# Attention and channel mix on one core: raw weight blocks move into spare tiles, the first queries come in two pieces, half of an early V product moves into other PSUM banks

## The chip, the cores and the metric

The kernel runs on one core of one Trainium2 chip. The core has five engines: PE (TensorE, matrix products), DVE (VectorE), ACT (ScalarE), POOL (GpSimd) and SP (SyncE, which issues the DMAs here). The metric is the device time of one execution in microseconds (us).

## What is computed

The inputs are q, k and v of 8 batches x 8 heads x 576 tokens x 64, and the weights of a channel mix. Both parts are float32.

```python
def _attn_ref(q, k, v):
    # rotate(x): rotary embedding, x1*cos - x2*sin and x1*sin + x2*cos over the halves of the 64
    q_rot, k_rot = (rotate(q), rotate(k))
    scores = scale * np.matmul(q_rot, k_rot.transpose(0, 1, 3, 2))
    scores = scores - np.max(scores, axis=-1, keepdims=True)
    attn = np.exp(scores)
    attn = attn / (np.sum(attn, axis=-1, keepdims=True) + 1e-09)
    return np.matmul(attn, v).astype(np.float32)

def _moe_ref(x, mu_k, mu_r, w_k, w_v, w_r):      # x: the heads side by side, 8 x 576 x 512
    x_prev = np.concatenate([np.zeros((B, 1, D), dtype=np.float32), x[:, :-1, :]], axis=1)
    xk = mu_k * x + (1.0 - mu_k) * x_prev
    xr = mu_r * x + (1.0 - mu_r) * x_prev
    k = np.maximum(xk @ w_k, 0.0)                # w_k: 512 x 1024
    v = k * k @ w_v                              # w_v: 1024 x 512
    r = 1.0 / (1.0 + np.exp(-(xr @ w_r)))        # w_r: 512 x 512
    return (r * v).astype(np.float32)
```

The weights reach the kernel as 64-bit numbers; it turns them into a high and a low float32 part itself.

## The kernel before, in words

**Attention.** Two heads make a pair, four pairs a batch, 32 pairs in all. For a pair, `plan_rope` loads keys (`xk`, 128x576, in two versions) and queries (`xq`, 128x640, in two versions) into tiles `nat`, multiplies them with the table `turn` in two products and adds them up into `kh` and `qh`. For the first nine pairs ("plain") this is all; later pairs get a high and a low part of both (`kh`, `kl`, `qh`, `ql`). `plan_unit` makes the scores in five units of 128 query columns: PE writes a tile `s` of two PSUM banks for each head (L431; the fifth unit has one tile), DVE takes the negated maximum `nm` (L440), ACT the exponentials into `p` with their sums (L444), and DVE transposes `p` in place (L447). `plan_ratio` makes the reciprocals of the sums, `rs` and `rw`. `plan_values` multiplies with V: 144 products per pair into two tiles `av` that are taken from the `s` family (L500), then 8 that spread the reciprocals (L506). `plan_total` copies these out with ACT (`rp`), multiplies with DVE (L531) and gets the head outputs `xT0` and `xT1`, one per half of the tokens.

PSUM has eight banks: three `s` tiles of two banks, and two `acc` tiles of one bank for the products of the channel mix.

**Weights.** `plan_convert` turns one block of 128x512 weights into its two parts. It loads the raw 64-bit block (`raw`, L339), ACT takes two signed parts of the top bits (`we`, `wm`, L345), DVE or POOL subtracts them (`wm<-we,wm`), ACT scales the middle bits (`we`, L351), POOL adds them (`wm<-wm,we`), ACT or DVE casts to the high part (`wk_h`, `wr_h`, `wv_h`, L312 or L314), and DVE or POOL subtracts for the low part (`wk_l`, `wr_l`, `wv_l`). There are 8 blocks of w_k, 4 of w_r and 8 of w_v, and one tile each of `raw`, `we` and `wm`. All the products, sums and differences with two SBUF inputs are recorded by the helper `combine`, so they have one line, L308.

**Channel mix.** For each batch and each half of the tokens, `plan_mix` mixes a pair's output with that of the token before into `mxf` (L571 or L569, then L574) and splits it into `mxh` and `mxl`; `plan_product` sums three products per pair or block into `acc` (L599 to L601); `plan_key`, `plan_gate` and `plan_value` square, gate and store.

**Order.** Every step is an `op` with a rank. `Plan.issue` keeps, for each engine, a list of steps whose inputs and tiles are there, always takes the one of the lowest rank, and so fixes the order of instructions of every engine when the program is built. Ranks come from a table of numbers: `R` for kinds of steps, `PB` and `EARLY` for the first pairs, `WORDS` for the weight blocks, `MB` for the batches; the `B_` numbers say how readily DVE takes a step that ACT or POOL could do, and `WAIT` how much a step of DVE or POOL that needs the port they share is put off while the other engine holds it. `BUFS` has the number of tiles of each family. A tile's next user waits for its last one.

Of the kernel before, what the change touches and what calls it, by code (L numbers as in the profile page):

```python
# [25 lines left out]
R = dict(k=41.29, q=43.11, v=-208.71, cs=-1094.85, ld=858.21, rope0=735.67, rope1=1324.78, rope2=-1784.84,  # L26
         split0=-295.59, split1=1862.14, u0=-14.6, u1=-12.59, u2=0.4, u3=-11.84, u4=-9.27, mx=-84.96, ex=99.42,
         rz=-275.08, rs=-668.43, dg=-117.58, bd=451.61, tr=-238.29, ev=349.84, av=10.21, av2=287.22, tot=-501.88,
         bor=-905.72, m0=174.53, mh=-2.54, mk=-24.02, mr=-14.79, ms=1.64, tp=850.66, rc=-602.82, mx1=-206.82,
         mx2=-1085.1, mx3=812.05, mg=3.33, mv=0.11, dr=-1034.03, key0=1074.87, key1=-426.54, key2=117.33,  # L30
         gate0=-493.48, gate1=383.07, wk0=120.98, wk1=45.04, wr0=-1131.23, wr1=-1623.73, wv0=98.26, wv1=1824.21)
# [15 lines left out]
WORDS = dict(wk=(-412.27, 471.27, -302.28, -396.61, -1095.29, -563.8, -1080.79, -139.77), wr=(-436.28, -440.01,
             -795.2, 242.23), wv=(-475.45, -213.94, -422, -856.83, -795.63, -590.27, 613.81, -729.62))
CY = 12
CUTS = (0, 6, 12, 18)  # L50
WAIT = 10.29
BUFS = dict(nat=2, kh=2, kl=2, qh=2, ql=2, vs=1, pt=2, s=3, nm=6, sums=2, rs=2, rw=1, rp=2, xT0=4, xT1=4, last=5, raw=1, we=1, wm=1, mxf=2, mxh=5, mxl=5, acc=2, hr=2, kkh=8, kkl=8, rt=3)
# [206 lines left out]
def rope_attention_channel_mix(ctx, tc, qt, kt, v, cs, mu, w_k, w_v, w_r, out):  # L259
# [72 lines left out]
    def plan_convert(t, src, hi, lo):  # L332
        d = {}
        s_w, s_e, s_m = Slot("raw"), Slot("we"), Slot("wm")

        def load():
            words = sb.tile([P, 513, 2], U32, tag="raw", name="raw", bufs=BUFS["raw"])
            quarters = words.rearrange("p n w -> p (n w)").bitcast(I16)
            nc.sync.dma_start(quarters[:, 1:2049], src)  # L339
            d["middle"] = words[:, 0:512, 1]  # L340
            d["top"] = quarters.rearrange("p (n w) -> p n w", w=4)[:, 1:513, 0]

        def signed(n, scale):
            d[n] = sb.tile([P, 512], I32, tag="w" + n, name="w" + n, bufs=BUFS["w" + n])
# [6 lines left out]
        e = op("A", t, act(512) + 30, lambda: A.mul(d["e"], d["middle"], 2.0 ** -13), [m], [s_w, s_e])  # L351
# [17 lines left out]
    def plan_rope(t, d, n, src, plain, pi):  # L369
# [4 lines left out]
        def load():  # L374
            m["x"] = sb.tile([P, 2, SQ], F32, tag="nat", name="x" + n, bufs=BUFS["nat"])
            m["c"], m["s"] = m["x"][:, 0, 0:w], m["x"][:, 1, 0:w]
            nc.sync.dma_start(m["x"][:, :, 0:w], src)
# [4 lines left out]

        ld = dma(t + R["ld"], P * 8 * w, load, [], [slot])
        ms = op(two(w, B_ROPE), t + lead("rope0", pi), 0, lambda e: combine(e, m["s"], m["s"], turn[:, 1, 0:w], ALU.mult), [ld] + tables["cs"], [slot])
        mc = op(two(w, B_ROPE), t + lead("rope1", pi), 0, lambda e: combine(e, m["c"], m["c"], turn[:, 0, 0:w], ALU.mult), [ld] + tables["cs"], [slot])
        sh = d["s" + n + "h"] = Slot(n + "h")
        if plain:
            r = op(two(w, B_ROPE), t + lead("rope2", pi), 0, lambda e: combine(e, f32(part(n + "h")), m["c"], m["s"], ALU.add), [ms, mc], [slot, sh])
            d[n], d["s" + n] = [r], [sh]
            return  # L390
# [24 lines left out]
    def plan_unit(t, d, c):  # L415
# [17 lines left out]
        m = op("T", t, (8 if d["plain"] else 6) * (120 + 12), products, d["q"] + d["k"], slots + d["sq"] + d["sk"], ("row" if c < 4 else "full", (8 if d["plain"] else 12) * len(heads)))  # L433
# [47 lines left out]
    def plan_values(t, d):  # L481


        w, slots = {}, [Slot("s"), Slot("s")]
# [4 lines left out]
        def at(a, x, c0):  # L489
            return w[a % 2][(up, dn)[x], a // 2, c0:c0 + Q]  # L490

        def values(b0, b1):
            if b0 == 0:
                for half in range(2):
                    w[half] = ps.tile([P, 2, 512], F32, tag="s", name="av", bufs=BUFS["s"])
# [22 lines left out]
        for half in range(2):  # L518
            plan_total(t, d, half, w, slots[half], o)

    def plan_total(t, d, half, w, slot, o):
# [3 lines left out]
        def copied():  # L525
            w["r", half] = sb.tile([P, 2, N // 2], F32, tag="rp", name="rp", bufs=BUFS["rp"])
            A.copy(w["r", half], w[half][:, :, 256:256 + N // 2])  # L527

        def total():
            x = d["x", half] = sb.tile([P, N + 1], F32, tag=f"xT{half}", name=f"xT{half}", bufs=BUFS[f"xT{half}"])  # L530
            V.tensor_tensor(out=x[:, 1:N + 1].rearrange("p (c n) -> p c n", c=2), in0=w[half][:, :, 0:N // 2], in1=w["r", half], op=ALU.mult)  # L531
# [10 lines left out]
        o = op("A", t + lead("rc", d["pi"]) + 0.1 * half, act(288) + 60, copied, [o], [slot, s_r])  # L542
        o = op("V", t + lead("tot", d["pi"]) + 0.1 * half, dve(288) + 30, total, [o], [slot, s_r, sx])
# [223 lines left out]
```

## Time and profile before

| | us |
|---|---|
| median of 3 runs | 992.77 (991.27 to 993.28) |
| the profiled execution | 991.33 |
| its span, first to last instruction | 989.6 |
| PE busy | 928.9 |
| DVE busy | 772.8 |
| ACT busy | 569.9 |
| POOL busy | 509.0 |

The span is what the profiler saw of the profiled execution; the 1.7 us to its own time lie around it. Busy times are sums over the span. What an engine waited for is inferred from the semaphores. The granted clock of PE is a share of full speed. A score unit or a weight product stands in the trace as two matmuls for each float32 instruction, and some records can be missing.

### The profile page before, as it was taken

Reading aid. Unit: us, or ns where it says so; the run is one execution under the profiler, and the core shown is the slowest. Engines: PE = TensorE matmul, PEld = TensorE weight load, DVE = VectorE, ACT = ScalarE, POOL = GpSimd, SP = SyncE. Lnnn points to the kernel's source line nnn. Section 1 sums busy time; section 2 is a strip of 40 time slices with the busy share of each in tenths; the row PEclk is TensorE's granted clock in tenths of the full one; section 3 lists DMA queues with packets and bytes.
Section 4 is the critical chain, followed back from the end, with each engine's and each line's share of the span. In section 5 each row is a group of like instructions: output and inputs, shape, how many; then the busy total and the mean of one; then the engine's idle time right before and its main releaser. Section 6 shows DMA issues by size and latency. Waiting matters only on the chain.

```text
span 989.6 us, 34384 instructions
## 1 busy us (share of the span) xinstructions
PE 928.9 (94%) x15134; PEld 821.1 (83%) x15134; DVE 772.8 (78%) x1248; ACT 569.9 (58%) x1394; POOL 509.0 (51%) x547
## 2 busy tenths in 40 slices
PE   2676789999999999999999999999999999999998
PEld 1344568888988999889988998988988999899998
DVE  5978789997786969788796969888696869874652
ACT  4655578355674747465574747566564737543343
POOL 6647677465653647465563647455463637131211
PEclk9867779999999999999999999999999999999999
DMA  7336532323333222233333222233322222111000
GB/s 254 123 114 217 179 121 93 126 101 112 112 112 112 97 78 101 70 106 112 112 107 105 94 92 79 90 110 107 118 107 84 86 100 78 59 62 57 20 25 25
DMA packets 30453, 100.38 MB, mean 101 GB/s; under 512 B 3040, under 2 KB 11232, under 8 KB 26208
## 3 DMA queue, kind: packets, MB, share of 16 engines
q1 hardware_dynamic: 30304, 98.19, 28.5%
q8 instruction: 118, 1.93, 0.8%
q14 instruction: 31, 0.25, 0.1%
HBM read 88.74 MB, written 9.44 MB: 99 GB/s over the span
## 4 chain that ended last, share of the span: by engine, by line
PE 82%; DVE 8%; ACT 4%; issue 2%; DMA 2%; POOL 1%; SPq 0%; DVEq 0%; ACTq 0%; POOLq 0%
PE acc L599 19%; PE av L500 16%; PE s L431 15%; PE acc L600 15%; PE acc L601 15%; DVE nm L440 2%; DVE mxf L574 2%; ACT p L444 1%; DVE p L447 1%; DMA raw<-in_w_k 1%; PE av L506 1%; DMA xk<-in_kt 1%; DMA raw<-in_w_v 1%; ACT rt L646 1%; DVE xq L308 1%
## 5 line engine op out<-in xcount | busy, mean ns | idle before, releaser
L444 ACT ACTIVATE p<-s,nm 128x576 f32<-128x576 f32 x288 | 211.7, 739 | 104.2 <-DVE nm L440 102.9
L440 DVE TENSOR_REDUCE nm<-s 128x1 f32<-128x576 f32 x288 | 202.2, 735 | 14.6 <-PE s L431 14.0
L447 DVE STREAM_TRANSPOSE p<-p 128x576 f32<-128x576 f32 x288 | 208.2, 752 | 2.5 <-ACT p L444 2.0
L500 PE MATMUL av<-p,values 32*64 32x144 f32 x9216 | 179.6, 293 | 13.9 <-issue 9.8
L500 PEld LDWEIGHTS av<-p,values 32*64 32x64 f32 x9216 | 151.7, 133 | 34.3 <-issue 25.6
L431 PE MATMUL s<-kh,qh 64*128 64x288 f32 (+1 forms) x738 | 145.3, 433 | 35.7 <-ACT p L444 16.7
L599 PE MATMUL acc<-mxh,wk_h 128*128 128x288 f32 x512 | 162.7, 318 | 1.7 <-ACT hr L616 1.5
L599 PE MATMUL acc<-kkh,wv_h 128*128 128x288 f32 x512 | 158.6, 310 | 4.1 <-DVE rt L655 4.0
L601 PE MATMUL acc<-mxh,wk_l 128*128 128x288 f32 x512 | 152.4, 298 | 1.9 <-DVE wk_l L308 1.9
L600 PE MATMUL acc<-mxl,wk_h 128*128 128x288 f32 x512 | 152.4, 298 | 0.0
L600 PE MATMUL acc<-kkl,wv_h 128*128 128x288 f32 x512 | 151.3, 296 | 0.0
L601 PE MATMUL acc<-kkh,wv_l 128*128 128x288 f32 x512 | 151.0, 295 | 0.0
L431 PEld LDWEIGHTS s<-kh,qh 64*128 64x128 f32 (+1 forms) x738 | 80.3, 207 | 83.6 <-ACT p L444 26.6
L308 POOL TENSOR_TENSOR mxl<-mxf,mxh 128x288 fp32r<-128x288 f32 x87 | 78.0, 903 | 74.9 <-ACT mxh L312 33.9
L308 POOL TENSOR_TENSOR kkl<-hr,kkh 128x288 fp32r<-128x288 f32 x99 | 87.6, 890 | 56.3 <-ACT kkh L312 45.0
L599 PEld LDWEIGHTS acc<-mxh,wk_h 128*128 128x128 f32 x512 | 97.0, 189 | 19.6 <-issue 13.6
L599 PEld LDWEIGHTS acc<-kkh,wv_h 128*128 128x128 f32 x512 | 96.1, 188 | 17.5 <-issue 11.5
L655 DVE TENSOR_TENSOR rt<-acc,rt 128x288 f32<-128x288 f32 x64 | 29.0, 453 | 101.5 <-PE acc L601 99.5
L527 ACT COPY rp<-av 128x288 f32<-128x288 f32 x64 | 22.4, 402 | 145.7 <-PE av L506 145.7
L538 POOL COPY last<-xT 128x1 f32<-128x1 f32 x32 | 6.9, 217 | 191.0 <-DVE xT L531 190.9
L601 PEld LDWEIGHTS acc<-mxh,wk_l 128*128 128x128 f32 x512 | 97.4, 190 | 2.1 <-DVE wk_l L308 2.1
L600 PEld LDWEIGHTS acc<-mxl,wk_h 128*128 128x128 f32 x512 | 97.4, 190 | 0.4
(86 smaller groups left out, 1921.5 us busy)
## 6 DMA issues: line engine op xcount, KB each, us to landing
values<-in_v SPq DMA_DIRECT2D x32, 1152.0 KB, 5.6
xq<-in_qt SPq DMA_DIRECT2D x32, 640.0 KB, 5.2
xk<-in_kt SPq DMA_DIRECT2D x32, 576.0 KB, 4.2
out_dram<-rt SPq DMA_DIRECT2D x64, 144.0 KB, 1.8
raw<-in_w_k SPq DMA_DIRECT2D x8, 512.0 KB, 3.6
raw<-in_w_v SPq DMA_DIRECT2D x8, 512.0 KB, 3.6
raw<-in_w_r SPq DMA_DIRECT2D x4, 512.0 KB, 4.2
turn<-in_cs SPq DMA_DIRECT2D x1, 640.0 KB, 4.9
```

The lines of the kernel that those rows point to most:

```text
L308: (V if e == "V" else G).tensor_tensor(out=out, in0=a, in1=b, op=op)
L431: T.matmul(w[x][:, h, 0:H], lhsT=kind(d[q][r, c * P:(c + 1) * P]), rhs=kind(d[k][r, h * H:(h + 1) * H]), start=i == 0, stop=i == len(todo) ...
L440: V.tensor_reduce(out=w["nm", x], in_=w[x][:, :, 0:H], op=ALU.max, axis=AX.XY, negate=True)
L444: A.activation(out, w[x][:, :, 0:H].rearrange("p a (b n) -> p a b n", n=32), AF.Exp, bias=w["nm", x], scale=1.0, accum_out=d["sums"][:, pl ...
L447: V.transpose(queries(d, place), queries(d, place))
L500: T.matmul(at(a, x, 0), lhsT=d["vf"][g, b * P + x * D:b * P + x * D + D], rhs=d["pt"][g, b, x * Q:x * Q + Q], start=b == 0, stop=b == NB - 1)
L527: A.copy(w["r", half], w[half][:, :, 256:256 + N // 2])
L574: V.scalar_tensor_tensor(out=x["f"], in0=d["x", half][:, 1:1 + n], scalar=mu_t[:, m:m + 1], in1=x["f"], op0=ALU.mult, op1=ALU.add)
L599: T.matmul(w["a"], lhsT=w_h[:, i, sl], rhs=x["h"], start=(i == 0), stop=False)
L600: T.matmul(w["a"], lhsT=w_h[:, i, sl], rhs=x["l"], start=False, stop=False)
L601: T.matmul(w["a"], lhsT=w_l[:, i, sl], rhs=x["h"], start=False, stop=(i == count - 1))
L655: o = op("V", t + R["dr"], dve(n), lambda: V.tensor_tensor(out=x["r"], in0=w["a"], in1=x["r"], op=ALU.mult), [done, o], [s_a, s_r])
```

## The change

There are three changes in the code, and a new table of numbers.

1. `plan_convert` takes its raw block from the tile family `ql` and its first signed part from `kl`, which the plain pairs leave unused and of which there are two each; `raw` and `we` are gone, and `wm` has two tiles. So two blocks can be under way.
2. The queries of the first pair are loaded in two pieces, columns 0 to 127 and 128 to 639, with their own products and sums. A unit of a plain pair asks for the pieces that it reads (`d["q"][:c + 1]`).
3. For the first four pairs, the V product of the second half of the tokens goes to the two `acc` tiles instead of a second `s` tile. ACT's copy and DVE's multiplication of that half become two each, one per bank.

```diff
-R = dict(k=41.29, q=43.11, v=-208.71, cs=-1094.85, ld=858.21, rope0=735.67, rope1=1324.78, rope2=-1784.84,
+R = dict(sg=146.09, k=35.07, q=51.6, v=-92.97, cs=-1440.03, ld=485.93, rope0=775.97, rope1=1341.24, rope2=-1593.82,
...
-WAIT = 10.29
-BUFS = dict(nat=2, kh=2, kl=2, qh=2, ql=2, vs=1, pt=2, s=3, nm=6, sums=2, rs=2, rw=1, rp=2, xT0=4, xT1=4, last=5, raw=1, we=1, wm=1, mxf=2, mxh=5, mxl=5, acc=2, hr=2, kkh=8, kkl=8, rt=3)
+WAIT = 1.297e+06
+BUFS = dict(nat=2, kh=2, kl=2, qh=2, ql=2, vs=1, pt=2, s=3, nm=6, sums=2, rs=2, rw=1, rp=2, xT0=4, xT1=4, last=5, wm=2, mxf=2, mxh=5, mxl=5, acc=2, hr=2, kkh=8, kkl=8, rt=3)
...
-        s_w, s_e, s_m = Slot("raw"), Slot("we"), Slot("wm")
+        s_w, s_e, s_m = Slot("ql"), Slot("kl"), Slot("wm")
...
-            words = sb.tile([P, 513, 2], U32, tag="raw", name="raw", bufs=BUFS["raw"])
+            words = sb.tile([P, 513, 2], U32, tag="ql", name="raw", bufs=BUFS["ql"])
...
-        e = op("A", t, act(512) + 30, lambda: signed("e", 1.0), [o], [s_w, s_e])
-        m = op("A", t, act(512) + 30, lambda: signed("m", -1.0), [o], [s_w, s_m])
+        e = op("A", t, act(512) + 130, lambda: signed("e", "kl", 1.0), [o], [s_w, s_e])
+        m = op("A", t, act(512) + 130, lambda: signed("m", "wm", -1.0), [o], [s_w, s_m])
...
+        def multiplied(e, i, c0, c1):
+            x = m["x"][:, i, c0:c1]
+            combine(e, x, x, turn[:, i, c0:c1], ALU.mult)
+
+        def added(e, c0, c1):
+            out = f32(part(n + "h")) if c0 == 0 else f32(d[n + "h"])
+            combine(e, out[:, c0:c1], m["c"][:, c0:c1], m["s"][:, c0:c1], ALU.add)
...
+        cuts = (0, P, w) if pi == 0 and n == "q" else (0, w)
+        for c0, c1 in zip(cuts, cuts[1:]):
+            u = c1 - c0
+            late = R["sg"] if c0 else 0
+            ld = dma(t + R["ld"] + late, P * 8 * u, lambda c0=c0, c1=c1: load(c0, c1), [], [slot])
...
+            if plain:
+                d[n].append(op(two(u, B_ROPE), t + lead("rope2", pi) + late, 0, lambda e, c0=c0, c1=c1: added(e, c0, c1), [ms, mc], [slot, sh]))
...
-        w, slots = {}, [Slot("s"), Slot("s")]
+        w = {}
+        alone = d["pi"] < 4
+        slots = [Slot("s")] + ([Slot("acc"), Slot("acc")] if alone else [Slot("s")])
...
-            return w[a % 2][(up, dn)[x], a // 2, c0:c0 + Q]
+            return w[a % 2][a // 2][(up, dn)[x], c0:c0 + Q]
...
-            A.copy(w["r", half], w[half][:, :, 256:256 + N // 2])
+            for i, r in banks():
+                A.copy(w["r", half][:, i], r[..., 256:256 + N // 2])
+
+        def banks():
+            return enumerate(w[half]) if apart else [(slice(0, 2), w["s", half])]
...
+            x = x[:, 1:N + 1].rearrange("p (c n) -> p c n", c=2)
+            for i, r in banks():
+                V.tensor_tensor(out=x[:, i], in0=r[..., 0:N // 2], in1=w["r", half][:, i], op=ALU.mult)
```

What the new ranks do to the order is seen on the engines themselves. First SP, the queue that issues the loads, from its first DMA on. Before:

```order
L339 DMA raw<-in_w_r 128x2048
L680 DMA turn<-in_cs 128x1280
L680 DMA mu_t<-in_mu 128x8
L377 DMA xk<-in_kt 128x2x576
L377 DMA xq<-in_qt 128x1280
L407 DMA values<-in_v 128x2304
L339 DMA raw<-in_w_r 128x2048
```

After:

```order
L339 DMA raw<-in_w_r 128x2048
L706 DMA turn<-in_cs 128x1280
L706 DMA mu_t<-in_mu 128x8
L339 DMA raw<-in_w_r 128x2048
L378 DMA xk<-in_kt 128x2x576
L378 DMA xq<-in_qt 128x2x128
L421 DMA values<-in_v 128x2304
L378 DMA xq<-in_qt 128x2x512
```

The second raw block now goes ahead of the first keys, and the larger piece of the first queries goes behind the first values.

Second POOL, its first twelve products, sums and differences. Before:

```order
L308 TENSOR_TENSOR xk<-xk,turn 128x576
L308 TENSOR_TENSOR wm<-wm,we 128x512
L308 TENSOR_TENSOR xq<-xq,turn 128x640
L308 TENSOR_TENSOR qh<-xq 128x640
L308 TENSOR_TENSOR wm<-wm,we 128x512
L308 TENSOR_TENSOR xq<-xq,turn 128x640
L308 TENSOR_TENSOR qh<-xq 128x640
L308 TENSOR_TENSOR xk<-xk,turn 128x576
L308 TENSOR_TENSOR kh<-xk 128x576
L308 TENSOR_TENSOR wm<-wm,we 128x512
L308 TENSOR_TENSOR xq<-xq,turn 128x640
L308 TENSOR_TENSOR wr_l<-wm,wr_h 128x512
```

After:

```order
L308 TENSOR_TENSOR wm<-wm,we 128x512
L308 TENSOR_TENSOR xk<-xk,turn 128x576
L308 TENSOR_TENSOR wr_l<-wm,wr_h 128x512
L308 TENSOR_TENSOR wm<-we,wm 128x512
L308 TENSOR_TENSOR xq<-xq,turn 128x512
L308 TENSOR_TENSOR qh<-xq 128x128
L308 TENSOR_TENSOR wm<-wm,we 128x512
L308 TENSOR_TENSOR xq<-xq,turn 128x640
L308 TENSOR_TENSOR wr_l<-wm,wr_h 128x512
L308 TENSOR_TENSOR qh<-xq 128x640
L308 TENSOR_TENSOR wm<-wm,we 128x512
L308 TENSOR_TENSOR wm<-we,wm 128x512
```

POOL now has seven steps of weight blocks among its first twelve, where it had four, and the first sum of queries that PE needs (`qh`) is its sixth step instead of its fourth.

Third PE, from its first instruction; one row of the order is one product, and rows alike are counted with x. Before:

```order
L431 MATMUL s<-kh,qh 128x288 x32
L500 MATMUL av<-p,values 64x144 x144
L506 MATMUL av<-rw,first_row 64x144 x8
L431 MATMUL s<-kh,qh 128x288 x16
L500 MATMUL av<-p,values 64x144 x48
L431 MATMUL s<-kh,qh 128x288 x2
L500 MATMUL av<-p,values 64x144 x96
L506 MATMUL av<-rw,first_row 64x144 x8
L599 MATMUL acc<-mxh,wk_h 128x288
```

After:

```order
L445 MATMUL s<-kh,qh 128x288 x32
L520 MATMUL av<-p,values 64x144 x48
L445 MATMUL s<-kh,qh 128x288 x4
L520 MATMUL av<-p,values 64x144 x96
L526 MATMUL av<-rw,first_row 64x144 x8
L445 MATMUL s<-kh,qh 128x288 x14
L520 MATMUL av<-p,values 64x144 x48
L445 MATMUL s<-kh,qh 128x288 x4
L520 MATMUL av<-p,values 64x144 x96
L526 MATMUL av<-rw,first_row 64x144 x8
```

The V product of the first pair is now cut once by a unit of scores, and no product of the channel mix (L599, now L625) stands between the early pairs.

## Rows read from the trace of the kernel before

**Rows 1.** The page, its first part: busy us, share of the span, instructions.

```profile
PE 928.9 (94%) x15134; PEld 821.1 (83%) x15134; DVE 772.8 (78%) x1248; ACT 569.9 (58%) x1394; POOL 509.0 (51%) x547
```

**Rows 2.** Busy time by stretch; columns as in the header line.

```profile
core 0: us, PE busy (x) PEld busy (x) DVE busy (x) ACT busy (x) POOL busy (x), PEclk, DMA share, GB/s
0.00:128.80 128.80, 79.41 (x1379) 54.12 (x1379) 95.84 (x136) 69.89 (x137) 80.06 (x73) 0.79 0.50 176
128.80:989.60 860.80, 849.52 (x13759) 766.98 (x13756) 676.95 (x1112) 500.01 (x1257) 428.93 (x475) 1.00 0.26 90
8.80:130.10 121.30, 80.42 (x1382) 54.67 (x1384) 95.75 (x136) 66.66 (x135) 80.23 (x67) 0.77 0.48 168
```

**Rows 3.** PE's waits up to 128.8: us in total, times, longest.

```profile
PE s L431 <- POOL qh L308: 16.5, 1, 16.5
PE s L431 <- ACT p L444: 14.9, 11, 2.5
```

**Rows 4.** PE's longest wait from 128.8 to the end.

```profile
PE acc L599 <- DVE rt L655: 4.2, 7, 1.3
```

**Rows 5.** SP's timeline, two raw loads: start us, us, engine, line, operation.

```profile
41.76 0.33 SPq L339 DMA_DIRECT2D raw<-in_w_k  x1
...
49.97 0.33 SPq L339 DMA_DIRECT2D raw<-in_w_k  x1
```

**Rows 6.** POOL's waits from 9 to 130.2.

```profile
POOL wm L308 <- ACT we L351: 14.8, 6, 4.1
...
POOL wm L308 <- ACT wm L345: 4.2, 4, 1.9
POOL rs L471 <- ACT p L444: 4.1, 1, 4.1
POOL kh L308 <- PE s L431: 4.0, 2, 2.9
```

**Rows 7.** DVE's timeline: the residue of the fourth pair's mixed input.

```profile
133.64 1.01 DVE L308 TENSOR_TENSOR mxl<-mxf,mxh 128x288 fp32r<-128x288 f32 x1
```

**Rows 8.** Timeline from 81 to 85: DVE and POOL at the same time.

```profile
81.23 1.92 POOL L308 TENSOR_TENSOR xq<-xq,turn 128x640 f32<-128x640 f32 x1 [2.60 <-DMA xq<-in_qt]
81.66 2.17 DVE L308 TENSOR_TENSOR xq<-xq,turn 128x640 f32<-128x640 f32 x1
...
83.10 1.85 POOL L308 TENSOR_TENSOR wm<-wm,we 128x512 int32<-128x512 int32 x1
```

**Rows 9.** Timelines of POOL, then DVE: steps that were not held up.

```profile
26.29 1.26 POOL L308 TENSOR_TENSOR wm<-wm,we 128x512 int32<-128x512 int32 x1
27.52 1.53 POOL L308 TENSOR_TENSOR xq<-xq,turn 128x640 f32<-128x640 f32 x1
...
64.64 0.80 POOL L308 TENSOR_TENSOR mxl<-mxf,mxh 128x288 fp32r<-128x288 f32 x1 [3.84 <-ACT mxh L312]
...
94.31 1.40 POOL L308 TENSOR_TENSOR xk<-xk,turn 128x576 f32<-128x576 f32 x1
...
47.99 0.69 DVE L308 TENSOR_TENSOR wm<-we,wm 128x512 int32<-128x512 int32 x1 [0.17 <-ACT wm L345]
...
63.29 0.51 DVE L574 SCALAR_TENSOR_TENSOR mxf<-xT,mu_t,mxf 128x288 f32<-128x288 f32 x1
...
124.17 0.76 DVE L308 TENSOR_TENSOR xk<-xk,turn 128x576 f32<-128x576 f32 x1
...
130.02 0.81 DVE L308 TENSOR_TENSOR xq<-xq,turn 128x640 f32<-128x640 f32 x1
```

**Rows 10.** Timeline from 8.6 to 17: the first keys, queries and product.

```profile
8.72 0.76 DVE L308 TENSOR_TENSOR xk<-xk,turn 128x576 f32<-128x576 f32 x1 [1.96 <-DMA xk<-in_kt]
8.79 1.95 POOL L308 TENSOR_TENSOR xk<-xk,turn 128x576 f32<-128x576 f32 x1 [7.17 <-DMA xk<-in_kt]
10.19 1.22 DVE L308 TENSOR_TENSOR xq<-xq,turn 128x640 f32<-128x640 f32 x1 [0.71 <-DMA xq<-in_qt]
...
16.54 0.85 PE L431 MATMUL s<-kh,qh 64*128 64x288 f32 x2 [16.54 <-POOL qh L308]
```

**Rows 11.** PE's timeline from 129: one unit of scores.

```profile
129.79 1.24 PE L431 MATMUL s<-kh,qh 64*128 64x288 f32 x8 [0.29 <-DVE xT L531]
```

More of the change, by code (lines that the diff above doesn't have):

```diff
@@ L25 @@
 PLAIN = 9
-R = dict(k=41.29, q=43.11, v=-208.71, cs=-1094.85, ld=858.21, rope0=735.67, rope1=1324.78, rope2=-1784.84,
[L27 to L31, printed above, removed]
@@ L372, in plan_rope, with load @@
         slot, w, m = Slot("nat"), src.shape[-1], {}
[L374 to L377, printed above, removed]
+        def load(c0, c1):
+            if c0 == 0:
+                m["x"] = sb.tile([P, 2, SQ], F32, tag="nat", name="x" + n, bufs=BUFS["nat"])
+                m["c"], m["s"] = m["x"][:, 0, 0:w], m["x"][:, 1, 0:w]
+            nc.sync.dma_start(m["x"][:, :, c0:c1], src[:, :, c0:c1])
         def part(name):
@@ L381, in part @@
             return d[name]
[L383 to L386 removed]
+        def multiplied(e, i, c0, c1):
[4 more added lines that the diff above has]
+            combine(e, out[:, c0:c1], m["c"][:, c0:c1], m["s"][:, c0:c1], ALU.add)
+        sh = d["s" + n + "h"] = Slot(n + "h")
+        d[n], d["s" + n] = [], [sh]
+        cuts = (0, P, w) if pi == 0 and n == "q" else (0, w)
[3 more added lines that the diff above has]
+            ld = dma(t + R["ld"] + late, P * 8 * u, lambda c0=c0, c1=c1: load(c0, c1), [], [slot])
+            ms = op(two(u, B_ROPE), t + lead("rope0", pi) + late, 0, lambda e, c0=c0, c1=c1: multiplied(e, 1, c0, c1), [ld] + tables["cs"], [slot])
+            mc = op(two(u, B_ROPE), t + lead("rope1", pi) + late, 0, lambda e, c0=c0, c1=c1: multiplied(e, 0, c0, c1), [ld] + tables["cs"], [slot])
+            if plain:
+                d[n].append(op(two(u, B_ROPE), t + lead("rope2", pi) + late, 0, lambda e, c0=c0, c1=c1: added(e, c0, c1), [ms, mc], [slot, sh]))
         if plain:
[L388 to L389 removed]
             return
@@ L431, in products @@
                         T.matmul(w[x][:, h, 0:H], lhsT=kind(d[q][r, c * P:(c + 1) * P]), rhs=kind(d[k][r, h * H:(h + 1) * H]), start=i == 0, stop=i == len(todo) - 1)
-        m = op("T", t, (8 if d["plain"] else 6) * (120 + 12), products, d["q"] + d["k"], slots + d["sq"] + d["sk"], ("row" if c < 4 else "full", (8 if d["plain"] else 12) * len(heads)))
+        m = op("T", t, (8 if d["plain"] else 6) * (120 + 12), products, (d["q"][:c + 1] if d["plain"] else d["q"]) + d["k"], slots + d["sq"] + d["sk"], ("row" if c < 4 else "full", (8 if d["plain"] else 12) * len(heads)))
         for x in heads:
@@ L494, in values @@
                 for half in range(2):
-                    w[half] = ps.tile([P, 2, 512], F32, tag="s", name="av", bufs=BUFS["s"])
+                    if half and alone:
+                        w[half] = [ps.tile([P, 512], F32, tag="acc", name="av", bufs=BUFS["acc"]) for _ in range(2)]
+                        continue
+                    w["s", half] = ps.tile([P, 2, 512], F32, tag="s", name="av", bufs=BUFS["s"])
+                    w[half] = [w["s", half][:, i] for i in range(2)]
             for b in range(b0, b1):
@@ L518, in plan_values, with plan_total @@
         for half in range(2):
-            plan_total(t, d, half, w, slots[half], o)
-    def plan_total(t, d, half, w, slot, o):
+            plan_total(t, d, half, w, slots[half:half + 1] if not alone else (slots[:1], slots[1:])[half], o, alone and half == 1)
+    def plan_total(t, d, half, w, slots, o, apart):
         s_r = Slot("rp")
@@ L540, in border @@
                 G.tensor_copy(xT[:, 0:1], d["last"])
-        o = op("A", t + lead("rc", d["pi"]) + 0.1 * half, act(288) + 60, copied, [o], [slot, s_r])
-        o = op("V", t + lead("tot", d["pi"]) + 0.1 * half, dve(288) + 30, total, [o], [slot, s_r, sx])
+        o = op("A", t + lead("rc", d["pi"]) + 0.1 * half, act(288) + 60 + 160 * apart, copied, [o], slots + [s_r])
+        o = op("V", t + lead("tot", d["pi"]) + 0.1 * half, dve(288) + 30 + 130 * apart, total, [o], slots + [s_r, sx])
         if half == 0:
```

44 lines of the change are left out of this document (24 added, 20 removed).

## The prediction

> **What bounds the kernel now.** I read the page first, then the span cut in two, then who waits for whom in the first part, then single instructions there. PE is busy for 928.9 of 989.6 us [rows 1], so a change can win only where PE idles, or where its clock is low. Cut at 128.8, where the V product of the fourth head pair ends [rows 2]: before the cut PE is idle for 128.8 - 79.4 = 49.4 us and its mean granted clock is 0.79; behind it, in 860.8 us, it is idle for 11.3 at clock 1.00. The second part is a full PE, whose largest kind of wait there, for DVE's last products, sums to 4.2 us [rows 4]. The first part is a ramp, and the reader is to see that PE waits in it first for the first pair's queries (16.5), then, again and again, for the exponentials of scores (14.9) [rows 3]. No engine is full in it: DVE is busy for 95.8 of 128.8, POOL for 80.1, ACT for 69.9 [rows 2].
>
> Two resources tie these engines together. One raw weight block is converted at a time, and the next may be loaded only when the last has been read: two raw loads stand 8.2 us apart, 41.76 and 49.97 [rows 5], and twenty blocks at that pace are 164 us. POOL, which has a part in every block, sits idle for 41.1 of the 121.3 us between 8.8 and 130.1 [rows 2]; 14.8 + 4.2 of it are waits for ACT's steps of a block, 4.1 for the exponentials (row sums), 4.0 for PE to be done with a key tile [rows 6]. The other is that DVE and POOL hinder each other. At 81.66 DVE starts a 128x640 product that takes 2.17, and 0.81 elsewhere; POOL's 128x640 product, 1.92 long, began at 81.23, and the 128x512 sum behind it takes 1.85, and 1.26 elsewhere [rows 8, 9]. The excess of DVE, 1.36, is close to what POOL still had to do (81.23 + 1.92 - 81.66 = 1.49). So I count products and sums with two SBUF inputs of the two engines as one queue, each at the duration that it has when not held up [rows 9].
> The Trainium skill ("SBUF — State Buffer", section "SBUF: two separate sides") has the same rule: the port pair that GpSimd and VectorE share is an exclusive lock, and the later one fully blocks. It speaks against this change, which moves work between the two engines and adds some. Without the rule one would sum POOL by itself; with it, the sum is the one below.
>
> **The change part by part.**
> First product: an extra raw block of 512 KB now goes ahead of the keys, and the queries come as 128 and, behind the values, 512 columns. Keys landed at 8.72 and the 640 KB of queries at 10.19 [rows 10], 435 KB per us; so the keys land 1.2 later, at 9.9. POOL then has the key product (1.40 to 1.95), a weight residue and a weight difference (1.26 each), the product of the 512 columns (four fifths of 1.53) and the sum of the 128 (a fifth of that) before PE may start [rows 9, 10]: 9.9 + 5.5 to 6.0 = 15.4 to 15.9, if nothing blocks; with one blocking by DVE (up to 1.4) 17.3. It was 16.54 [rows 10]. I take 0; the ends are -1 and +1. What the pieces gain, the raw block and POOL's new order take.
>
> The ramp: its end is the moment when PE gets the fourth pair's mixed input. DVE made it at 133.64 + 1.01 = 134.6 [rows 7]. I count the shared queue up to there, from the instruction orders (numbers before, then after), at those durations, kh priced as xk and qh as xq (same widths), DVE's residues as its 128x512 difference:
> POOL before: 30 weight steps x 1.26 = 37.8; 10 key steps x 1.40 = 14.0; 11 query steps x 1.53 = 16.8; 3 residues of mixed inputs x 0.80 = 2.4; 71.0 in all. After: 46 x 1.26 = 58.0; 9 x 1.40 = 12.6; 8 x 1.53 = 12.2 and 1.5 for the two pieces; 3 x 0.80 = 2.4; 86.7.
> DVE before: 17 weight steps x 0.69 = 11.7; 10 x 0.76 = 7.6; 9 x 0.81 = 7.3; 6 steps 288 wide x 0.51 = 3.1; 29.7. After: 8 x 0.69 = 5.5; 11 x 0.76 = 8.4; 6 x 0.81 = 4.9 and 1.7 for the pieces; 5 x 0.51 = 2.6; 23.1.
> So 100.7 becomes 109.8: 9.1 us more, because about three more blocks are under way or done by then. From 8.7, when the keys are there, to 134.6 are 125.9; the queue was empty for 25.2 of them. What becomes of these 25.2 decides. Of POOL's 41.1 idle, 27.1 are the four waits of [rows 6], and each loses its cause: with two raw blocks (tiles ql, two of kl, two of wm) a second block is ready when the first waits for ACT; with half of the V product in the two acc banks, scores keep two of three s tiles while it runs, so DVE has maxima and transposes to do there and PE frees keys sooner. I let 27.1/41.1 = 66% of the empty time go: 8.6 stay, and the ramp ends at 8.7 + 109.8 + 8.6 = 127.1, 7.5 earlier. Bounds: all 25.2 stay, 143.7 (9.1 later); none stays, 118.5 (16.1 earlier).
>
> PE at that point: after the change it has done 10 more rows of score products (all five units of the fifth pair, where before it had two) and three fewer weight products. Four such rows, eight matmuls in the trace, took 1.24 us [rows 11], so ten take 3.1; three weight products at the 0.155 that one of these eight takes are 0.4 or so: 2.7 us that need not be done later. Cover: PE was busy for 79.4 of 128.8 [rows 2], so it can take 2.7 more in 118 to 127; without cover the 2.7 are lost.
>
> At nothing: DVE's multiplication and ACT's copy of the half in acc banks become two of 144 columns each, four times; a 288-wide step of DVE takes 0.51 [rows 9], so what the split adds lies between 0 and 0.51 each, at most 2 us per engine for four pairs, hidden by DVE's 33 and ACT's 59 us of idle [rows 2]. The early k products can no longer start before the fourth pair; they are the three products less, counted above. ACT gets the steps of two to three blocks more by the cut, hidden by its 59 us of idle as well; without that cover each costs less than the 8.2 us in which a whole block now passes through all engines [rows 5], and the gain is gone. Behind the ramp the table moves only small numbers of steps between engines; PE idles for 11.3 there and may gain or lose 3.
>
> Sum on the profiled execution (991.33, span 989.6 and 1.7 around it): 991.33 - 7.5 - 2.7 = 981.1. The median of the runs is 992.77, 1.4 above, so 982.5.
>
> **The rivals.**
> (1) The queue is nearly never empty: 0 to 3 us stay, 13 to 16 earlier plus 2.7, so 974 to 977. For it: a second block always gives POOL something to do, and between two marks of the ramp DVE and POOL can overlap more than I count. Against it: the order is fixed when the program is built, and POOL follows PE and ACT in several places [rows 6].
> (2) The gain is handed back behind the ramp: PE starts sooner, and the mixing of inputs (DVE) and the last three w_v blocks are late. Half of the 10.2 lost gives 987.6. For it: DVE is 79% busy over the whole second part. Against it: five blocks were left there before, now three, and PE's waits there were small [rows 4].
> (3) No change: about a quarter of the 25.2 goes (6.3), and with the 2.7 this just pays for the 9.1 of added work: within 0.2%, 991 to 995. For it: POOL's list is longer by 15.7 us. Against it: the four waits are two thirds of its idle [rows 2, 6]. This is the case that the change does not do what it says: more in flight, nothing sooner.
> (4) Slower: POOL's longer list is the bound and its waits only change their names: POOL now does 32 instead of 21 weight differences and sums, while the keys and queries stand behind these in its queue. For it: POOL takes 1.26 for a step that DVE does in 0.69 [rows 9]. Against it: two blocks in flight are what takes POOL's longest waits away. If all 25.2 stay, the ramp ends 9.1 later, less 2.7: 999. It decides from the point where less than (9.1 - 2.7)/25.2 = 25% of the empty time goes. Before the change the queue was full for only 80% of the time; after it, it must be full for 85% to break even.
>
> **How the numbers follow.** Forecast, 977 to 988 around 982.5: 0.56. Rival 1: 0.15. Rival 2, at 986 to 991: 0.13. Rival 3: 0.07. Rival 4, 995 to 999: 0.09. The bounds of the first product and of PE's later waits add 1 and 3. The range 972 to 992 leaves out the best end of rival 1, half of rival 3 and rival 4. Faster by over 0.2% (2 us, about what a measurement of this kernel can tell from none): 0.84; within 0.2%: 0.07; slower: 0.09.
>
> **What would show it.** Right: first product between 15.5 and 17.5; raw loads in the ramp on average under 7 us apart; the fourth V product ending near 115 to 121 and PE without longer waits from about 127; POOL over 80% busy between 9 and 120, its wait for ACT's weight steps under 7 us; scores running between the pieces of a V product; PE idle behind the ramp still about 11. Wrong: POOL's waits as long as before, under scores' or ACT's name; a V product of the first pair that ends much later than 60 without the next ones catching up; new PE waits for mixed inputs or w_v behind 130.

## The result and the profile after the change

The changed kernel takes 977.43 us (median of four runs, 976.91 to 977.65), the kernel before 992.22 in the runs beside it; the ratio is 0.985, 95% interval 0.9833 to 0.9867. The forecast was 982.5 in 972 to 992: the right side, the gain 14.8 us and not 10.2. The profiled executions are 13.8 us apart (spans 989.6 and 975.8). One execution of a run below (e8) took 2146 us, more than twice as long as its others, and is left out of that run's time.

The page's first part answers to [rows 1], the stretches to [rows 2]. The cut is again the end of the fourth V product, now at 115.2:

```profile
PE 920.2 (94%) x15134; PEld 814.8 (83%) x15134; DVE 775.3 (79%) x1255; ACT 568.1 (58%) x1394; POOL 525.0 (54%) x551
```
```profile
0.00:115.20 115.20, 76.88 (x1377) 52.56 (x1377) 102.25 (x136) 77.56 (x159) 95.42 (x87) 0.85 0.59 206
115.20:975.80 860.60, 843.33 (x13758) 762.20 (x13758) 673.01 (x1120) 490.57 (x1236) 429.59 (x464) 1.00 0.26 89
9.00:120.00 111.00, 80.95 (x1399) 55.46 (x1399) 106.06 (x141) 77.81 (x165) 95.14 (x81) 0.85 0.57 202
```

The ramp is 13.6 us shorter and the rest as long as it was (860.6 and 860.8). In the rest PE is busy for 6.2 us less (849.5 to 843.3) and idle for 6.0 more (11.3 to 17.3). Between 9 and 120 DVE is now busy for 106.1 of 111 us, time in which POOL holds it up included, and POOL for 95.1; in the same stretch of the kernel before they were busy for 90.0 and 73.7.

PE's waits up to 120 (answer to [rows 3]), then two rows of before, up to 128.8, that belong beside them, and POOL's waits from 9 to 120 (to [rows 6]):

```profile
PE s L445 <- POOL qh L308: 17.7, 1, 17.7
PE s L445 <- ACT p L458: 11.0, 9, 2.6
PE s L445 <- DVE nm L454: 4.0, 1, 4.0
...
PE av L520 <- issue: 2.4, 3, 1.6
```
```profile
PE av L500 <- issue: 9.8, 6, 4.6
PE av L500 <- DVE p L447: 4.2, 2, 3.0
```
```profile
POOL wm L308 <- ACT we L351: 8.9, 5, 6.4
...
POOL wm L308 <- ACT wm L345: 2.7, 2, 1.8
POOL rs L485 <- ACT p L458: 2.0, 2, 1.2
```

PE waits less for the exponentials (14.9 to 11.0). Its gaps ahead of V products shrink by more: they were 9.8 + 4.2 us and are 2.4, or 3.1 with a shorter one that is not shown. POOL no longer waits for PE to be done with a key tile. Of its 8.9 us for `we`, 6.4 are one wait that ends at 8.04, ahead of the stretch:

```profile
8.04 1.26 POOL L308 TENSOR_TENSOR wm<-wm,we 128x512 int32<-128x512 int32 x1 [6.43 <-ACT we L351]
```

So between 9 and 120 POOL waits 2.5 + 2.7 us for ACT's weight steps, where it had waited 11.2 + 4.2. SP's raw loads from 8 to 125, of before and of after:

```profile
L339 SPq DMA_DIRECT2D raw<-in_w_k x7: 327/328/328, 33.9 to 100.6; - x7
L339 SPq DMA_DIRECT2D raw<-in_w_v x5: 327/328/328, 57.0 to 124.9; - x5
L339 SPq DMA_DIRECT2D raw<-in_w_r x3: 327/328/328, 7.9 to 26.0; - x3
```
```profile
L339 SPq DMA_DIRECT2D raw<-in_w_v x8: 328/328/372, 16.0 to 119.3; - x8
L339 SPq DMA_DIRECT2D raw<-in_w_k x8: 327/328/333, 29.2 to 87.7; - x8
L339 SPq DMA_DIRECT2D raw<-in_w_r x2: 328/331/334, 7.9 to 20.6; - x2
```

One block of before and two of after had left ahead of 8. So before, 16 of 20 blocks had left by 125, with 8.4 us between them ((124.9 - 7.9)/14); now all 20 have, with 6.6 ((119.3 - 7.9)/17). The fourth pair's mixed input, which ended at 134.6 [rows 7], is POOL's now and ends at 122.3:

```profile
L308 POOL TENSOR_TENSOR mxl<-mxf,mxh x1: 791/791/791, 121.5 to 121.5; 128x288 fp32r<-128x288 f32 x1
```

### The profile page after: what moved, and what is told of

Read it like the earlier page. It is cut to its first block, busy times and chain, and to the rows that moved or that the text cites. A ratio compares the mean times of both kernels' runs of the same rounds, so it can differ in the third digit from the quotient of the medians.

```text
span 975.8 us, 34418 instructions
## 1 busy us (share of the span) xinstructions
PE 920.2 (94%) x15134; PEld 814.8 (83%) x15134; DVE 775.3 (79%) x1255; ACT 568.1 (58%) x1394; POOL 525.0 (54%) x551
## 4 chain that ended last, share of the span: by engine, by line
PE 74%; DVE 18%; ACT 3%; DMA 2%; issue 2%; POOL 1%; SPq 0%; DVEq 0%; ACTq 0%
PE acc L625 18%; PE av L520 15%; PE acc L626 14%; PE acc L627 14%; PE s L445 12%; DVE nm L454 5%; DVE p L461 4%; DVE mxf L600 3%; DVE xk L308 2%; ACT p L458 2%; DMA xq<-in_qt 1%; DMA xk<-in_kt 1%; DVE rt L681 1%; PE av L526 1%; DVE xq L308 1%
## 5 line engine op out<-in xcount | busy, mean ns | idle before, releaser
L454 DVE TENSOR_REDUCE nm<-s 128x1 f32<-128x576 f32 x288 | 202.7, 737 | 13.4 <-PE s L445 12.9
L520 PE MATMUL av<-p,values 32*64 32x144 f32 x9216 | 177.6, 293 | 2.7 <-issue 2.4
L520 PEld LDWEIGHTS av<-p,values 32*64 32x64 f32 x9216 | 150.9, 134 | 22.5 <-issue 19.4
L625 PE MATMUL acc<-mxh,wk_h 128*128 128x288 f32 x512 | 160.9, 314 | 3.4 <-ACT hr L642 3.2
L625 PE MATMUL acc<-kkh,wv_h 128*128 128x288 f32 x512 | 158.3, 309 | 4.5 <-DVE rt L681 4.3
L625 PEld LDWEIGHTS acc<-mxh,wk_h 128*128 128x128 f32 x512 | 96.1, 188 | 21.7 <-issue 14.1
L625 PEld LDWEIGHTS acc<-kkh,wv_h 128*128 128x128 f32 x512 | 96.1, 188 | 18.1 <-issue 11.1
L308 POOL TENSOR_TENSOR mxl<-mxf,mxh 128x288 fp32r<-128x288 f32 x77 | 69.7, 913 | 72.4 <-DVE mxh L314 49.4
L548 ACT COPY rp<-av 128x288 f32<-128x288 f32 (+1 forms) x68 | 22.8, 389 | 135.3 <-PE av L526 134.8
L600 DVE SCALAR_TENSOR_TENSOR mxf<-xT,mu_t,mxf 128x288 f32<-128x288 f32 x128 | 95.6, 755 | 6.2 <-ACT mxf L595 5.2
```

The costliest lines, as they stand in the source:

```text
L308: (V if e == "V" else G).tensor_tensor(out=out, in0=a, in1=b, op=op)
L454: V.tensor_reduce(out=w["nm", x], in_=w[x][:, :, 0:H], op=ALU.max, axis=AX.XY, negate=True)
L520: T.matmul(at(a, x, 0), lhsT=d["vf"][g, b * P + x * D:b * P + x * D + D], rhs=d["pt"][g, b, x * Q:x * Q + Q], start=b == 0, stop=b == NB - 1)
L548: A.copy(w["r", half][:, i], r[..., 256:256 + N // 2])
L600: V.scalar_tensor_tensor(out=x["f"], in0=d["x", half][:, 1:1 + n], scalar=mu_t[:, m:m + 1], in1=x["f"], op0=ALU.mult, op1=ALU.add)
L625: T.matmul(w["a"], lhsT=w_h[:, i, sl], rhs=x["h"], start=(i == 0), stop=False)
```

## The experiments

Four theories. D: two blocks in flight fill the queue that DVE and POOL share. V: the free third tile of scores does it. T: the table of ranks does it, whatever the buffers; later O: the parts pay only in the order that the new ranks make. Q: the first product. Each run was timed beside the kernel before, and each time is a median; "the cut" is the end of the fourth V product, read as above.

### Each part undone, planned anew: e1_one_block, e2_half_in_s, e3_whole_query

The main lines of the three edits (the last words of e1's are a note on the tiles):

```diff
e1  -        s_w, s_e, s_m = Slot("ql"), Slot("kl"), Slot("wm")
    +        s_w, s_e, s_m = Slot("raw"), Slot("we"), Slot("wm")   # raw=1, we=1, wm=1
e2  -        alone = d["pi"] < 4
    +        alone = False
e3  -            cuts = (0, P, w) if pi == 0 and n == "q" else (0, w)
    +            cuts = (0, w)
```

> The changed kernel with the first part undone: one weight block at a time again (raw block, and both ScalarE parts, in one buffer each of their own), all else and the new table kept. Theory D (depth: two blocks in flight fill the queue that VectorE and GpSimd share, and that is most of the gain): raw loads again 8 us apart where they are now 6.0 on the average from 29 to 59 us, GpSimd's waits for ScalarE's weight steps back from 12.6 to about 20 us, the fourth V product 7.5 to 13.6 us later than 115.2, so 985 to 991. Rival V (the V half in the other banks is most of the gain): at most 3 us lost, 977.5 to 980.5. Rival T (the table of ranks is most of it, whatever the buffers): the same 977.5 to 980.5.

> The changed kernel with the third part undone: both halves of an early V product in tiles s again, all else and the new table kept. Theory D: scores can no longer run between the pieces, TensorE's gaps before V products go from 2.4 back towards 9.8 us, but VectorE and GpSimd stay nearly full, so 1 to 4 us lost: 978.5 to 981.5. Rival V: 7 us or more lost, 984.5 to 991, with VectorE's busy time from 10 to 100 us under 90%. Rival T: under 1 us, 976.5 to 978.5.

> The changed kernel with the second part undone: the first pair's queries in one load and one turn each. The first product should come 1 to 2 us later than 17.75 (a whole 640-column sum is 1.5 us on GpSimd, the 128-column one 0.84). Theory D, in which the shared queue of VectorE and GpSimd sets the ramp and the split only adds instructions to it: within 1 us, 976.5 to 978.5. Rival Q (all of the ramp hangs on the first product): the delay goes through to the end, 978.5 to 979.5.

Measured: 1014.82 (ratio 1.0236, 1.0212 to 1.0261), 991.78 (0.9991, 0.9982 to 0.9999) and 990.04 (0.9967, 0.9954 to 0.9979). Each part taken away costs 12.6 us or more, together far more than the whole gain, and all three miss every range (e2 that of V by 0.8). The stretches of e1 and e3, each up to its cut and behind:

```profile
107.40:250.00 142.60, 120.73 (x1718) 94.90 (x1718) 115.37 (x169) 78.54 (x183) 78.87 (x79) 0.84 0.34 115
250.00:1012.70 762.70, 745.41 (x12043) 682.48 (x12041) 582.17 (x977) 420.66 (x1062) 364.15 (x391) 1.00 0.25 84
```
```profile
0.00:115.60 115.60, 71.50 (x1377) 48.71 (x1378) 106.04 (x137) 84.05 (x170) 101.53 (x88) 0.87 0.59 209
115.60:988.20 872.60, 850.14 (x13758) 767.13 (x13758) 673.33 (x1127) 478.58 (x1218) 424.66 (x460) 0.99 0.26 87
```

In e1 the cut comes at 107.4, earlier than in the changed kernel: attention runs ahead. PE is then idle for 21.9 us in the 142.6 behind it, 10.5 of them in waits for exponentials and 7.1 in waits for parts of weight blocks, and its mean clock there is 0.84. In e3 the ramp is as long as in the changed kernel (115.6), and all of the loss lies behind it (872.6 for 860.6). A loss so far from the edit is not the edit's own: the planner, given one small difference, wrote another order for the whole kernel. These three runs price a part together with a new order.

### Parts done to the kernel before, planned anew: e4_conv_alone, e12_code_old_ranks

e4 is the edit of e1 the other way round; e12 has all three edits with the table of before (`sg=146.09`, `WAIT = 10.29`).

> The kernel before with the first part alone: two weight blocks in flight, the table of ranks of before. Theory D: the queue of VectorE and GpSimd fills, 7 to 11 us gained on 992.2: 981 to 985. Rival V: 990 to 993, as scores still can't run beside the V product and TensorE is the one that waits. Rival T: 991 to 996, since the order was made for one block in flight and the earlier weight steps push attention's steps back.

> All three edits of the code, planned with the ranks and the holding rule of before (the delay of the second query piece as in the changed kernel). Theory O (the edits pay only with ranks fitted to them): slower than before, 995 to 1030, as the first edit alone gave 1030. Theory D (the edits bring the gain, and the fourth experiment failed for lack of the free score tile): 978 to 988.

Measured: 1029.99 (1.0386, 1.0364 to 1.0408) and 1017.14 (1.0247, 1.0231 to 1.0264). With the old ranks the edits lose 37 and 24 us: e4 misses every range, e12 lies in that of O. e4's cut and rest:

```profile
0.00:138.60 138.60, 79.72 (x1379) 55.35 (x1379) 108.20 (x139) 80.00 (x157) 98.43 (x87) 0.88 0.51 179
138.60:1025.00 886.40, 854.82 (x13759) 768.40 (x13756) 689.90 (x1158) 468.13 (x1197) 407.03 (x451) 1.00 0.25 85
```

Of the 35.4 us of span that e4 loses, 9.8 are in the ramp and 25.6 behind it. That two blocks in flight bring the gain by themselves, whatever the order (D, as first put), is refuted.

### The same parts with the order held

To price a part without a new order, I wrote down which step each engine takes, one after the other, in the changed kernel (in e8 and e13: in the kernel before), and had the planner follow that list. The second piece of the code stands in e9 and e10 alone: where tiles run out, the earliest step that is ready goes ahead.

```diff
+        todo = {e: [i for x, i in ORDER if x == e] for e in "TVAGS" if e not in FREE}
...
+                    if e in todo:
+                        i = todo[e][0] if todo[e] else None
+                        if i not in {r[1] for r in queue}:
+                            break
+                        todo[e].pop(0)
...
+                _, e, i = min(left_over)
+                todo[e].remove(i)
+                todo[e].insert(0, i)
```

**e7_whole_query_held** (edit of e3, in the first piece's places):

> The changed kernel with the first pair's queries in one piece, each engine's order held: the whole step stands where the first piece's stood, and the second piece's steps are gone (8 rows of VectorE differ, 5 of GpSimd, none of TensorE and ScalarE). First product 19 to 20 us in place of 17.75. Theory O (the 12.6 us of the third experiment were the order): 976.5 to 979. Rival Q (the late first product goes through everything): 985 to 991 as in the third experiment.

977.93 (0.9859, 0.9845 to 0.9872): the same as the changed kernel. Q falls, and the split of the queries is worth nothing that can be measured; the first product is not even later without it:

```profile
17.25 3.25 PE L543 MATMUL s<-kh,qh 64*128 64x288 f32 x10 [17.25 <-POOL qh L405]
```

**e8_before_two_held** (edit of e4; ORDER of before, SP free):

> The kernel before with two weight blocks in flight, the order of the four compute engines held to that of before to the last row: only the raw loads leave earlier. Theory D in its simplest form (a raw block that is there early is what the queue lacked): 984 to 988. Theory O (two blocks pay only with an order that uses them; the loads of before took under half of the 8.2 us between them): 990 to 992.5, with GpSimd's waits for ScalarE's weight steps little changed at 15 to 20 us.

988.05 (0.9956, 0.9943 to 0.9969), 3.8 us faster by the medians and 4.4 by the ratio: at the edge of D's range, and 2 us below O's. The raw loads leave earlier (the eight of w_k from 26.7 to 122.3, before from 33.9 to 133.0), but the cut hardly moves (128.2); of the 2.7 us of span gained, idle time gives none (60.7 before, 62.2 now) and busy time 4.2 (928.9 to 924.7), with a mean clock of 0.83 in place of 0.79 in the ramp:

```profile
0.00:128.20 128.20, 75.75 (x1379) 51.51 (x1379) 98.66 (x136) 68.27 (x138) 81.50 (x74) 0.83 0.53 183
```

**e9_one_block_held** (edit of e1; SP free):

> The changed kernel with one weight block at a time, the order of every engine's instructions held to that of the changed kernel as near as one block allows: TensorE's is the same to the last row, VectorE, ScalarE and GpSimd take only those weight steps later that one block forces (24 on ScalarE, 8 on GpSimd, 1 on VectorE), the raw loads follow. Theory D (two blocks in flight fill the shared queue): 984 to 990, fourth V product 7 to 13 us later than 115.2. Theory O (what a part is worth lies in the order that the ranks were fitted to; the 38 us of the first experiment came from the new order, not from the missing buffers): under 3 us lost, 976.5 to 980.5. Two blocks in the order of before gave 3.9 us, so something between would say that buffers and order need each other.

1070.89 (1.079, 1.0773 to 1.0807), 93 us more than the changed kernel, where O said under 3 and D at most 13. ACT's waits, then PE's, from 9 to 190:

```profile
ACT we L449 <- DMA raw<-in_w_k: 31.6, 7, 11.7
ACT we L449 <- DMA raw<-in_w_v: 23.1, 5, 9.6
ACT we L449 <- DMA raw<-in_w_r: 14.3, 3, 6.8
```
```profile
PE s L549 <- ACT p L562: 71.6, 17, 9.9
```

ACT stands for 69 us before raw blocks that have not landed, the exponentials stand behind it, and PE waits 71.6 us for them. ACT's queue is in order here as the Trainium skill has it ("PSUM — Partial Sum Buffer", section "Engine vs sequencer instructions": a strict first-in, first-out queue). So the order of the changed kernel can't be had without the second block: it puts a block's first steps early because its load is early.

**e10_half_in_s_held** (edit of e2):

> The changed kernel with both halves of the early V products in tiles s, the order held to that of the changed kernel as near as the tiles allow (16 score rows on TensorE that ran between the pieces of a V product move behind it, and what hangs on them). Theory V (the free third tile of scores is worth 7 us or more, as the 14.4 us of the second experiment say): 984 to 992. Theory O: only those score rows come later, 1 to 4 us: 978.5 to 981.5.

993.11 (1.0, 0.9988 to 1.0012): 15.7 us, all of the gain, for 16 rows of scores that move behind the V products. O's 1 to 4 us are refuted, and even V's 984 to 992 is passed by a little. The stretches, and PE's waits up to the cut:

```profile
0.00:126.70 126.70, 79.82 (x1369) 54.33 (x1369) 99.39 (x130) 77.36 (x154) 96.05 (x87) 0.82 0.55 186
126.70:991.80 865.10, 846.34 (x13767) 764.57 (x13766) 674.84 (x1121) 490.76 (x1236) 429.19 (x464) 1.00 0.26 89
```
```profile
PE s L549 <- ACT p L562: 12.7, 11, 2.6
PE av L624 <- ACT p L562: 8.3, 4, 2.8
```

The V product now waits 8.3 us for exponentials, a wait that the changed kernel does not have, since the last scores of a pair start later; DVE is idle for 27.3 us of the ramp (126.7 - 99.4), and was for 13.0 in the changed kernel. The ramp ends 11.5 later, and 4.5 are lost behind.

So D, V and O each fall as single causes. With the new order, both the second block and the free tile are needed; without it the second block alone brings a loss (e4) or 4 us (e8), and all three edits a loss (e12). How much the V half alone would be worth in the order of before was not tried: there the first k products hold the `acc` tiles while V products run.

### What bounds the ramp now: e11_casts_on_scalar, e13_before_casts, e14_seven_residues

ORDER held; in the list, four roundings of weight blocks go from VectorE to ScalarE (e11; the five in the ramp of before in e13), and in e14 seven weight residues from GpSimd to VectorE as well. Nothing else in the lists differs: 4, 5 and 11 steps change their engine and keep their place.

> The changed kernel, its order held, with the four roundings of weight blocks that VectorE does in the first 116 us (0.43 to 1.40 us each, 4.35 together) on ScalarE at the same places (0.62 each); TensorE and GpSimd unchanged to the last row. Theory F (after the change the full VectorE sets the ramp, busy 96% of 10 to 116 us): the ramp ends 2 to 4.4 us earlier, 973 to 975.5. Rival S (a weight step put ahead of an exponential delays the scores by as much): 976.5 to 978.5.

> The kernel before, its order held, with the five roundings of weight blocks that VectorE does ahead of the end of the fourth V product (0.40 to 1.62 us each, 3.3 together) on ScalarE at the same places. The same edit to the changed kernel gave 3.2 us. Theory F (VectorE is full only after the change; in the kernel before it is busy for 95.8 of 128.8 us and waits): within 1.2 us of before, 991 to 993. Rival W (the four us are saved wherever VectorE loses these roundings): 988 to 990.

> The changed kernel, its order held, with the four roundings on ScalarE as in the run at 974.25, and every second one of the first fourteen weight residues of GpSimd on VectorE at the same places (seven). Theory L (what sets the ramp is the queue that the two engines share, 109.8 us of work in the 113.5 from the keys to the fourth pair's mixed input): GpSimd loses 7 x 1.26 = 8.8, VectorE gains 7 x 0.69 = 4.8, the queue is 4.0 shorter, 970 to 973. Rival M (VectorE alone is the bound): it gets 4.8 us more to do, 976 to 980.

e11: 974.25 (0.9815, 0.9799 to 0.9831), faster than both kernels: 3.2 us below the changed one, of the 4.35 that the four roundings took there. e13: 992.92 (1.0004, 0.9993 to 1.0014), nothing. So VectorE's load bears on the ramp after the change and did not before it: both forecasts of theory F came true, and S and W fall. Whether it is VectorE's time or that of the port which it shares with GpSimd, these two runs can't tell, since such a rounding is held up by GpSimd too (next section). The cut of e11 is 2.5 us earlier, and behind it the kernel is what it was:

```profile
0.00:112.70 112.70, 73.06 (x1377) 49.96 (x1377) 98.25 (x132) 79.87 (x163) 95.68 (x87) 0.85 0.62 211
112.70:972.80 860.10, 843.42 (x13760) 762.45 (x13758) 675.15 (x1120) 489.89 (x1236) 428.24 (x464) 1.00 0.26 89
```

e14: 976.1 (0.9833, 0.9813 to 0.9853). The 4 us that a shorter shared queue should give didn't come; against e11 it is level or 2 us worse, which the intervals don't decide. From 0 to its cut at 114.7 POOL is busy for 8.5 us less than in e11 and DVE for 1.8 more:

```profile
0.00:114.70 114.70, 73.49 (x1377) 50.74 (x1377) 100.01 (x139) 79.62 (x164) 87.19 (x80) 0.85 0.61 208
```

So the sum of the two engines' work is not the limit by itself (L falls); M's 976 to 980 is touched at its lower end, which doesn't prove it. What holds e14 up is open: which of the seven stood ahead of a maximum or a transpose was not tried one by one.

## Why the prediction was right, step by step

**The empty time of the queue: the term whose size was off.** The count of work, 109.8 us, comes from the orders and stands. From 8.7 to the mixed input at 122.3 are 113.6, so by this count 3.8 us were empty, where I let 8.6 stay. That is 4.8 us, more than the forecast missed on the profiled executions (13.8 - 10.2 = 3.6). But what the count calls empty is a remainder: it adds up durations as if no two steps ever overlapped. Add up the timelines of both engines instead, the same kinds of steps, with time in which both engines are in one counted once. Then the queue was in use for 94.0 of the 125.9 us (counted: 100.7) and empty for 31.9 (25.2); now it is in use for 101.2 of 113.6 and empty for 12.4. So 61% of the empty time went, near the 66% that I took. What was mis-sized is the empty time itself, 31.9 and not 25.2, and the price of the added work, 7.2 and not 9.1: 31.9 - 12.4 - 7.2 = 12.3, by which the mixed input is earlier. Whether two steps share the port while they overlap, or only begin and end outside of it, the timelines don't tell.

The causes of the waits went as I said, for the most part. POOL is idle for 15.9 of 111 us, 43% of the 37.3 in the same stretch before:

```profile
9.00:120.00 111.00, 72.47 (x1085) 48.07 (x1093) 89.96 (x126) 62.55 (x128) 73.67 (x60) 0.77 0.47 164
```

The four waits of [rows 6], 23.5 us in that stretch, are 7.2 now, and those for ACT's weight steps 5.2, under the 7 that I named. The share was taken from POOL alone. DVE went from 90.0 to 106.1 us, and its waits for weight steps, 12.9 us in the first three rows (before, from 9 to 120), are down to the 0.2 of the last (after):

```profile
DVE wm L308 <- ACT wm L345: 8.7, 7, 3.2
...
DVE wk_h L314 <- POOL wm L308: 3.1, 2, 2.2
...
DVE wv_h L314 <- POOL wm L308: 1.1, 1, 1.1
```
```profile
DVE wk_h L314 <- POOL xT L562: 0.2, 1, 0.2
```

e10 shows what else keeps DVE there: without the scores beside the V product the gain is gone. e9 shows that the second block is needed as well. Two mechanisms that I named side by side work, in this order, only together.

**What the count left out.** It held only products and sums with two SBUF inputs. DVE's roundings, with one input, are held up too: 0.43 us when POOL does tiny steps (83.44), 1.40 when POOL's key product has begun (27.54 to 28.95).

```profile
27.54 1.41 POOL L308 TENSOR_TENSOR xk<-xk,turn 128x576 f32<-128x576 f32 x1
...
27.84 1.40 DVE L314 CAST wr_h<-wm 128x512 fp32r<-128x512 f32 x1
...
83.44 0.43 DVE L314 CAST wk_h<-wm 128x512 fp32r<-128x512 f32 x1 [0.17 <-POOL xT L562]
```

The excess, 0.97, is near what POOL still had to do, 1.11. The Trainium skill has a rule that would cover them ("SBUF — State Buffer", section "SBUF: two separate sides": an op of VectorE in a two-port mode contends for the lock as well); the durations agree, though no row says in which mode a rounding runs. e11 prices the four roundings, held up or not, at 3.2 us.

**The first product** came at 17.75, 0.25 outside my 15.5 to 17.5, and did no harm (e7). The keys landed 1.8 later than before, not 1.2 (DVE's first key product starts at 10.52, it was 8.72 [rows 10]).

```profile
17.75 2.76 PE L445 MATMUL s<-kh,qh 64*128 64x288 f32 x9 [17.75 <-POOL qh L308]
```

**PE's credit**, 2.7, follows from the order, and its cover held: PE is busy for 76.9 of 115.2. It counts at the first weight product behind the fourth pair's mixed input. That one starts at 123.52 and started at 134.71; ahead of it PE has done 180 matmuls of scores, ten rows more than the 160 of before, and 15 weight products, which were 18 (a weight product is one matmul in the trace, not two). At the V product's end there is next to no credit: 16 matmuls of scores more, and none of the 18 weight products, about 2.5 us against 2.4 (estimated at 0.155 and, for products back to back behind the ramp, 0.133 each).

**Behind the ramp** I expected PE to be idle for about 11, give or take 3; it is 17.3. Some stretches, first of before, then of after, say where:

```profile
128.80:200.00 71.20, 68.96 (x959) 56.30 (x957) 65.02 (x106) 48.99 (x118) 43.42 (x47) 0.95 0.33 109
...
400.00:600.00 200.00, 197.88 (x3383) 179.16 (x3382) 160.77 (x259) 116.46 (x295) 107.92 (x118) 1.00 0.29 99
600.00:800.00 200.00, 198.16 (x3373) 179.35 (x3372) 167.48 (x269) 123.72 (x314) 111.50 (x120) 1.00 0.28 98
```
```profile
115.20:186.40 71.20, 69.15 (x985) 57.69 (x986) 64.73 (x102) 47.32 (x119) 43.18 (x44) 1.00 0.33 110
...
386.40:586.40 200.00, 195.54 (x3364) 176.91 (x3363) 160.56 (x258) 114.39 (x290) 109.67 (x114) 1.00 0.29 99
586.40:786.40 200.00, 194.72 (x3360) 176.13 (x3359) 166.17 (x270) 121.23 (x308) 114.60 (x117) 1.00 0.28 97
```

In the last two, idle time grew from 2.1 + 1.8 to 4.5 + 5.3 us: the new order costs 5.8 in pairs far from any edit. Most of it is a wait that those 400 us did not have before:

```profile
PE s L445 <- ACT p L458: 4.0, 4, 1.2
```

Rival 2 (handed back) was right that something is, and wrong on the place: it expected mixed inputs and the last `w_v` blocks just behind the ramp. Just behind the ramp something is gained, for which I had no term either: the mean granted clock in the first 71.2 us was 0.95 and is 1.00, the full 2.4 GHz, and PE passes 985 matmuls in them, not 959. In the later 400 us it passes 32 fewer.

**The sum**, on the profiled executions: 11.2 (ramp, by PE's first weight product behind the mixed input) + 2.7 (credit) - 0.1 (what is left for all behind it) = 13.8. Forecast were 7.5 + 2.7 + 0. So the ramp's term was too small, and that the rest came to nothing is luck: the clock's gain and the new order's loss, neither of them forecast, about cancel. By the V product's end the same 13.8 are 13.6 + 0.2. Rival 1 came nearest by time (974 to 977). Its mechanism is shown by half: the queue is still empty for 12.4 us and not 0 to 3, but DVE and POOL do overlap more than I count. Rivals 3 and 4 needed POOL's longer list to be the bound; POOL is the less busy of the two engines.

## What to carry to other kernels

Where a program fixes the order, buffers and order are one thing: take a part away with the order held, or the price is that of a new order (e3 against e7: 12.6 us against 0.5). A shared resource is empty only when all its users leave it, so look at all of them, and measure the empty time on the timelines: elapsed time less the sum of the steps' durations is something else when steps overlap (25.2 against 31.9 us here). Once a ramp is filled, ask which engine is full now and give its smallest movable steps to one that is not: four roundings gave 3.2 us here, and nothing before the change.

## What the runs showed of the hardware

The same 15,134 matmuls keep PE busy for 920.2 us here, 916.5 in e11 and 939.0 in e1: orders of the same work differ by 22.5 us in it, and the low granted clocks lie in stretches in which PE waits again and again (mean 0.84 from 107.4 to 250 in e1, 1.00 behind).
